# Inverse transform: token blocks joined in pairs, the residual accumulated in PSUM by ScalarE, weight splits spread over more units

## Chip, cores and metric

One core of a Trainium2 chip runs the whole program. The metric is device time in microseconds (us) of one execution. A profiled execution gives, in addition, a trace of each engine: TensorE (PE, with its weight loads shown apart as PEld), VectorE (DVE), ScalarE (ACT), GpSimd (POOL) and SyncE (SP, which here only issues DMAs). Each engine works through its own queue strictly in the order in which the program was built; engines wait for each other through semaphores.

## Reference

A layer norm of x feeds two branches, and both are added to x:

```
x: [2048 tokens, 448]            xn = layernorm(x)
A = irfft2(rfft2(xn) * (w_r + 1j*w_i))          # 2-D Fourier filter over tokens and features
B = (relu(xn @ W_gate) * (xn @ W_up)) @ W_down  # 448 -> 1792 -> 448
out = x + A + B                                  # all float32
```

## The kernel before

**Precision and TensorE work.** All matmuls run in float16 with every float32 operand split into a high and a low part (three products for one). Splitting a tile takes one ScalarE instruction (high) and one VectorE instruction (low).

**Branch B** is the foreground. F = 1792 is cut into 14 slabs f of 128, in three groups of 5, 5 and 4; the tokens are cut into four chunks q of 512. A *gu unit* (f, q) multiplies chunk q with the gate and up slab f into a pair of PSUM banks (`gu`, two pairs): `gu_full` L797 on 128 rows, `gu_half` L804 for a leftover of 64 rows, of which two units (a unit and its mate) are done side by side at the end of the earlier one, into both units' banks. Then come ReLU (`gu_relu`, ScalarE L832), gate times up (`gu_times`, VectorE L836, which is what frees the PSUM pair) and the split of the product (L840, L844). After all slabs of a group have passed for a chunk, four *dn units* multiply the products with W_down (L868), each on one of two banks `dn`; ScalarE seeds the bank with x (`dn_seed`, L861) and takes the sum out again into x (`dn_post`, L872). The last four dn units are written out by hand in `dn_end` (L900, L879). Slabs of weights are loaded into staging buffers `wst` (8 of 128x512), squared and summed for a scale, and split by `w_hi` (ScalarE L746) and `w_lo` (VectorE L750) some units before their first use.

**Branch A** is the background. Tokens are 16 blocks n2 of 128 (token 16p + n2 sits in partition p). The forward half makes, per pair of blocks n2 and n2 + 8, a transform along the features and one along the tokens of a block (matmuls `f_dft` L414 and `f_sdft` L447), and combines the 16 blocks by four stages of butterflies on VectorE in 128x464 float32 tiles `y`. After the product with w, three stages of butterflies go back. Then, for p = 0..7, the **inverse runs** that the change rewrites:

- `bring(p)`: `stage4` (`bfly`, L453 to L478) joins two tiles into blocks p and p + 8, in two tiles `y`; `i_swap` (L648) has SP copy one row `row` into the tile and exchange its partition halves into a buffer `sw` by two DMAs (L586, L587; four buffers).
- `i_pair` (L592, L593) adds the exchanged side, once for each block.
- `i_mix` (L655) is an 8-point step along the features, `eight_a` and `eight_b` (L365 to L388): 16 VectorE instructions for each block. The forward half calls the same two functions on tiles that hold two blocks (128x928, called `eo` and `bw`).
- `i_hi` (ScalarE L667) and `i_lo` (VectorE L672) split the result into `vt`; `i_sdft` (L682) transforms along the tokens into a PSUM bank `fx` (there are two), `i_pqhi` and `i_pqlo` (L688, L691) split that.
- `i_ddft` (L705) transforms p and p + 8 along the features into both `fx` banks; a one-column ScalarE copy (`two_banks`, L398) goes first. `i_acc` (VectorE L719, two instructions of 128x224 for each block) scales the sums and adds them to x in `xy`, which frees the banks. `store` sends a block to HBM once both branches are in it. Blocks whose dn bank is seeded at that moment wait for `dn_post` (the set `seeded`).

One row of frequencies takes a path of its own: `row_dft` (PE L632), `row_hi2`/`row_lo2` (L623, L627), `row_ev` (VectorE L645), whose result the swaps need.

**What sets the order.** The opening is written out as a list. After it a loop over the units issues the foreground, and `run_bg` adds background steps from the list `bg`, each with a VectorE cost in us; a load factor is solved so that the background is used up by the unit that stands LASTGU before the last gu unit. `sched` and `gslot` place weight loads and splits a number of gu units ahead. The tile framework then orders each engine's queue by its own timing model and priorities.

Of the kernel before, what the change touches and what calls it, by code (L numbers as in the profile page):

```python
# [43 lines left out]
NSW = 4  # L44
LASTGU = 5
# [39 lines left out]
def _constants():  # L85
# [46 lines left out]
    for s in range(8):  # L132
        th = 2 * np.pi * (np.outer(kp, m + s) % D) / D
        o = slice(56 * (s // 2), 56 * (s // 2) + 56)
        c_id[64 * (s % 2):64 * (s % 2) + GW, :, o] = np.stack(
            _split(np.concatenate([g * np.cos(th), -g * np.sin(th)], axis=0)), axis=1)
# [7 lines left out]
def tile_gfnet_reglu(ctx: ExitStack, tc: tile.TileContext, x, xr, wgu, wd, wf, ident, c_fd, c_fm, c_im, c_row, c_id,  # L144
# [21 lines left out]
    xy = mt([128, 16, D], F32, "xy")  # L166
# [48 lines left out]
    def load_x(n2):  # L215
        nc.sync.dma_start(xy[:, n2, :], xv[:, n2, :])
# [9 lines left out]
    def load_w(f, g, eng=nc.sync):  # L226
        wst[f, g] = mt([128, 4, 128], F32, "wst", 8)
        eng.dma_start(wst[f, g], wgu[f, :, g])
# [219 lines left out]

    def bfly(a, b, p, sgn):
# [16 lines left out]
        th = 2 * np.pi * p / 16  # L466
        c, s = float(np.cos(th)), float(np.sin(th)) * sgn
        if abs(c) >= abs(s) - 1e-9:
            k, f = s / c, c
            V.scalar_tensor_tensor(t[:, :, 0], b[:, :, 1], k, b[:, :, 0], op0=OP.mult, op1=OP.add)  # L470
            V.scalar_tensor_tensor(t[:, :, 1], b[:, :, 0], -k, b[:, :, 1], op0=OP.mult, op1=OP.add)
        else:
            k, f = c / s, s
            V.scalar_tensor_tensor(t[:, :, 0], b[:, :, 0], k, b[:, :, 1], op0=OP.mult, op1=OP.add)
            V.scalar_tensor_tensor(t[:, :, 1], b[:, :, 1], k, b[:, :, 0], op0=OP.mult, op1=OP.subtract)
# [41 lines left out]
    def wsq_scale():  # L517
# [4 lines left out]
        V.tensor_scalar(fsc[:, 1:2], n, 2.0 ** -3 * 4.0 / (S * D), None, op0=OP.mult)  # L522
        V.reciprocal(fsc[:, 0:1], small[:, 19:20])

    inv = {}

    def open_inv():
        fwd.__exit__(None, None, None)
        state["ip"] = ip = ctx.enter_context(tc.tile_pool(name="inv", bufs=1))
        state["vt"] = [ip.tile([128, 2, NG, 64], F16, name=f"vt{i}") for i in range(2)]  # L530
        for v in state["vt"]:
            G.memset(v[:, :, :, GW:], 0.0)
        state["sw"] = [ip.tile([128, NG, 2, KC], F32, name=f"sw{i}") for i in range(NSW)]
# [49 lines left out]
    def swap(key):  # L583
        t = sw[key] = state["sw"][state.setdefault("swn", 0) % NSW]
        state["swn"] += 1
        nc.sync.dma_start(t[1:64], cur[key][65:128])  # L586
        nc.sync.dma_start(t[65:128], cur[key][1:64])  # L587

    def pair(key, sgn):
        u, t = cur[key], sw.pop(key)  # L590
# [61 lines left out]
    def i_pair(n2):  # L652
        pair(("U", n2), -1)

    def i_mix(n2):  # L655

        u = cur.pop(("U", n2))
        t, s = free.pop(0), free.pop(0)
        eight_a(u, s, u[:, 1:4])
        eight_b(t, s, u[:, 1:4], -1)  # L660
        free.extend((u, s))
        cur["Q", n2] = t

    def i_hi(n2):
        v = vt[n2] = state["vt"][state.setdefault("vn", 0) % 2]
        state["vn"] += 1
        A.activation(v[:, 0, :, 0:GW], cur["Q", n2].rearrange("p g c k -> p g (c k)"), AF.Copy, scale=fsc[:, 0:1])  # L667

    def i_lo(n2):
        ut = cur.pop(("Q", n2))  # L670
        v = vt[n2]
        V.scalar_tensor_tensor(v[:, 1, :, 0:GW], ut.rearrange("p g c k -> p g (c k)"), fsc[:, 0:1], v[:, 0, :, 0:GW],  # L672
                               op0=OP.mult, op1=OP.subtract)
        free.append(ut)

    def i_sdft(n2):
        ps = fx()
        v, m = vt[n2].rearrange("p a g k -> p a (g k)"), im_t[n2]
# [351 lines left out]
    for p in range(-1, 8):  # L1030
        if p >= 0:
            both(0.6, i_pqlo, p)
        if -1 < p < 6:
            bring(p + 2)
# [282 lines left out]
```

## Time and profile before

| | |
|---|---|
| Median of 3 runs | 447.38 us (447.23 to 448.21) |
| The profiled execution | 446.98 us |
| Its span, first to last instruction | 445.2 us |
| ScalarE busy | 239.5 us, 54%, 502 instructions |
| GpSimd busy | 35.7 us, 8% |
| Idle of VectorE before L836, in all | 7.6 us, waiting for ScalarE's ReLU |
| Idle of VectorE before L592, in all | 6.4 us, waiting for the DMAs of `row` and `sw` |
| SP issues of a swap (L586, L587) | 64, 0.73 and 0.71 us each in the middle |

The span is what the engines need, and the execution has 1.8 us around it. Where rows of the profile are shown, *busy* is the time an engine has at least one instruction in flight; an instruction's own duration is longer than the distance to the next one, since they overlap. A value in square brackets behind a row is the idle time in front of it, with what ended it.

### The profile page before, as it was taken

To read this page: it belongs to the slowest core of one execution; us is meant where nothing else is said; L and a number is where in the kernel's file an instruction comes from. 1 tells how busy PE (TensorE), PEld (TensorE's weight loads), DVE (VectorE), ACT (ScalarE), POOL (GpSimd) and SP (SyncE) were. 2 spreads that over 40 slices of the span, in tenths; PEclk is the share of its full clock that TensorE was granted. 3 is DMA by queue.
4 is the path that set the end of the run, shared out by engine and by line. 5 is a ranking of instruction groups with operands and counts; after the bars stand their busy time and mean duration, and the time that the engine had idled before them with its cause. 6 is when DMAs were issued, how large, how long until landed. Compare 5 with 4: busy or idle time off the path is not lost.

```text
span 445.2 us, 8321 instructions
## 1 busy us (share of the span) xinstructions
PE 433.0 (97%) x3009; PEld 209.7 (47%) x3009; DVE 391.0 (88%) x1077; ACT 239.5 (54%) x502; POOL 35.7 (8%) x89
## 2 busy tenths in 40 slices
PE   7999999999999999999999999989999989999996
PEld 2544444444454444444444444434555544554554
DVE  5988798997998899999999999699999979997343
ACT  5888484577468837616333573573552623625440
POOL 2320040040200040000000012010000000000000
PEclk9999999999999999999999999999999999999999
DMA  7839995050002362432202100200120111120112
GB/s 258 299 83 253 383 275 103 2 101 8 2 0 72 117 202 96 137 105 86 85 2 85 44 0 1 86 1 2 55 91 8 33 64 56 45 95 12 69 63 82
DMA packets 39512, 39.66 MB, mean 89 GB/s; under 512 B 18736, under 2 KB 35376, under 8 KB 39472
## 3 DMA queue, kind: packets, MB, share of 16 engines
q1 hardware_dynamic: 39472, 39.14, 28.8%
q8 instruction: 23, 0.38, 0.4%
q14 instruction: 17, 0.14, 0.1%
HBM read 24.25 MB, written 3.67 MB: 63 GB/s over the span
## 4 chain that ended last, share of the span: by engine, by line
DVE 51%; PE 34%; DMA 5%; issue 4%; ACT 3%; SPq 1%; POOL 1%; DVEq 0%; ACTq 0%
PE gu L797 18%; PE dn L868 9%; DVE g L836 5%; DVE h L844 4%; DVE wt L750 3%; DVE y L454 2%; DVE y L478 2%; DVE y L453 2%; DMA sw<-y 2%; DVE y L593 2%; DVE y L559 2%; DVE y L556 2%; DVE y L477 2%; DVE y L592 2%; PE fx L447 1%
## 5 line engine op out<-in xcount | busy, mean ns | idle before, releaser
L797 PE MATMUL gu<-T,wt 128*128 128x512 f16 (+1 forms) x1140 | 254.1, 375 | 0.4 <-DVE wt L750 0.4
L797 PEld LDWEIGHTS <-wt 128*128 128x128 f16 x1140 | 109.1, 98 | 132.2 <-issue 9.7
L868 PE MATMUL dn<-wdt,h 128*128 128x448 f16 x624 | 127.3, 353 | 0.0
L868 PEld LDWEIGHTS <-h 128*128 128x128 f16 x624 | 59.9, 98 | 57.2 <-issue 1.3
L840 ACT ACTIVATE h<-g 128x512 f16<-128x512 f32 x56 | 35.0, 627 | 91.8 <-DVE g L836 91.7
L836 DVE SCALAR_TENSOR_TENSOR g<-gu,g 128x512 f32<-128x512 f32 x56 | 38.2, 682 | 7.6 <-ACT g L832 7.6
L832 ACT ACTIVATE g<-gu 128x512 f32<-128x512 f32 x56 | 32.8, 585 | 19.3 <-PE gu L797 11.7
L844 DVE TENSOR_TENSOR h<-g,h 128x512 f16<-128x512 f32 x56 | 38.1, 682 | 5.6 <-ACT h L840 5.5
L872 ACT ACTIVATE xy<-dn,dsc 128x448 f32<-128x448 f32 x44 | 27.4, 625 | 23.4 <-PE dn L868 23.4
L861 ACT ACTIVATE dn<-xy,dinv 128x448 f32<-128x448 f32 x44 | 27.6, 632 | 11.5 <-DVE xy L719 10.9
L191 POOL PARTITION_ALL_REDUCE wm<-wm x15 | 10.2, 679 | 162.6 <-ACT junk L188 162.6
L746 ACT ACTIVATE wt<-wst,wsc 128x512 f16<-128x512 f32 x28 | 19.3, 713 | 3.5 <-DVE wsc L198 3.5
L750 DVE SCALAR_TENSOR_TENSOR wt<-wst,wsc,wt 128x512 f16<-128x512 f32 x28 | 20.5, 746 | 0.5 <-ACT wt L746 0.4
L804 PE MATMUL gu<-T,wt 64*128 64x512 f16 x112 | 16.9, 380 | 1.6 <-DVE g L836 1.5
L592 DVE TENSOR_TENSOR y<-y,sw 128x232 f32<-128x232 f32 x32 | 12.6, 393 | 6.4 <-DMA y<-row 3.2
L188 ACT ACTIVATE junk<-wst 128x512 bf16<-128x512 f32 x28 | 17.3, 619 | 0.4 <-DMA wst<-in_wgu 0.3
L719 DVE SCALAR_TENSOR_TENSOR xy<-fx,fsc,xy 128x224 f32<-128x224 f32 x32 | 12.2, 443 | 5.1 <-PE fx L705 5.0
L252 DVE BATCH_NORM_STATS2 bst<-y 128x6 f32<-128x448 f32 x16 | 9.5, 611 | 5.7 <-DMA y<-in_xr 5.7
L667 ACT ACTIVATE vt<-y,fsc 128x464 f16<-128x464 f32 x16 | 10.8, 676 | 6.6 <-DVE y L388 5.7
L453 DVE TENSOR_TENSOR y<-y,y 128x464 f32<-128x464 f32 x22 | 14.0, 637 | 0.3
L454 DVE TENSOR_TENSOR y<-y,y 128x464 f32<-128x464 f32 x22 | 13.9, 632 | 0.0
L682 PE MATMUL fx<-im,vt 128*128 128x128 f16 x192 | 12.0, 219 | 1.4 <-DVE xy L719 1.4
(147 smaller groups left out, 515.2 us busy)
## 6 DMA issues: line engine op xcount, KB each, us to landing
sw<-y SPq DMA_DIRECT2D x64, 114.2 KB
wst<-in_wgu SPq DMA_DIRECT2D x28, 256.0 KB
wf<-in_wf SPq DMA_DIRECT2D x16, 232.0 KB
y<-in_xr SPq DMA_DIRECT2D x16, 224.0 KB
xy<-in_x SPq DMA_DIRECT2D x16, 224.0 KB
out<-xy SPq DMA_DIRECT2D x15, 224.0 KB
wdst<-in_wd SPq DMA_DIRECT2D x14, 224.0 KB
fm<-in_c_fm SPq DMA_DIRECT2D x4, 256.0 KB
```

Source lines behind the costliest of these rows:

```text
L453: V.tensor_tensor(t, a, b, op=OP.add)
L454: V.tensor_tensor(d, a, b, op=OP.subtract)
L592: V.tensor_tensor(u[:, :, 0], u[:, :, 0], t[:, :, 1], op=o1)
L750: V.scalar_tensor_tensor(w[:, 4:8, :], st, sc, w[:, 0:4, :], op0=OP.mult, op1=OP.subtract)
L797: last["P"] = P.matmul(hps[f, q][:, g, cs], wt[f, g][:, a, :], Tq[q][:, b, cs], start=(start and i == 0), stop=(stop and i == len(seq) - 1 ...
L832: last["A"] = A.activation(g1s[f, q], hps[f, q][:, 0, :], AF.Relu, scale=2.0 ** -22).ins
L836: last["V"] = V.scalar_tensor_tensor(g1, hps[f, q][:, 1, :], 2.0 ** -22, g1, op0=OP.mult, op1=OP.mult).ins
L840: A.activation(ht[f, q][:, 0, :], g1s[f, q], AF.Copy)
L844: V.tensor_tensor(h[:, 1, :], g1s.pop((f, q)), h[:, 0, :], op=OP.subtract)
L861: A.activation(dps[n2][:, 0:D], xy[:, n2, :], AF.Copy, scale=dinv[:, g:g + 1])
L868: last["P"] = P.matmul(dps[n2][:, 0:D], ht[f, q][:, a, js], wdt[f][:, b, :], start=False, stop=(f == fs[-1] and a == 1), skip_group_check= ...
L872: last["A"] = A.activation(xy[:, n2, :], dps[n2][:, 0:D], AF.Copy, scale=dsc[:, g:g + 1]).ins
```

## The change

1. **Two blocks share a tile.** `i_join` writes both results of the last butterfly into one tile of 128x928 (blocks p and p + 8 side by side), which it takes from the ring of `wst` (now 4 buffers of 128x1024 for pairs of slabs, in place of 8 single ones). `i_swap`, `i_pair`, `i_mix`, `i_hi` then work on the pair; `i_lo` has still one instruction for each block. There are two swap buffers of double size.
2. **The residual goes through PSUM.** `i_ddft` has ScalarE put x, scaled by 1/`fsc[1]`, into the two `fx` banks; the matmuls add to it, and ScalarE takes the scaled sum out into `xy`. Each of the four instructions covers both blocks (128x448), for which `xy` is laid out so that p and p + 8 are neighbours. A pair with a block in `seeded` goes the old way (`fresh`).
3. `c_id` has its sine part 32 rows below the cosine part (padding in `vt`, one tile), and its scale takes a factor 8/7.
4. **Splits spread.** `w_hi`, `w_lo` and the next load are scheduled for half g at slot + g; LASTGU goes from 5 to 9. The list `bg` is written for pairs, with costs for them.

```diff
-LASTGU = 5
+LASTGU = 9
...
+    xy2 = mt([128, 8, 2, D], F32, "xy")
+    xy = [xy2[:, n2 % 8, n2 // 8] for n2 in range(16)]
...
+        if g == 0:
+            t = mt([128, 2, 4, 128], F32, "wst", 4)
+            wst[f, 0], wst[f, 1] = t[:, 0], t[:, 1]
         eng.dma_start(wst[f, g], wgu[f, :, g])
...
-    def i_swap(n2):
-        nc.sync.dma_start(cur["U", n2][64:65], row[n2:n2 + 1])
-        swap(("U", n2))
...
+    def i_join(p):
+
+        u = U[p] = mt([128, 2, 4, 128], F32, "wst", 4).rearrange(...)
+        a, b = cur.pop(("i3", 0, p)), cur.pop(("i3", 1, p))
+        o, d = (u[:, :, :, KC * i:KC * (i + 1)] for i in range(2))
...
+            t = free.pop(0)
+            f = rotate(t, b, p, -1)
+            V.scalar_tensor_tensor(o, t, f, a, op0=OP.mult, op1=OP.add)
+            V.scalar_tensor_tensor(d, t, -f, a, op0=OP.mult, op1=OP.add)
...
+    def i_swap(p):
+        u = U[p]
+        for i in range(2):
+            nc.sync.dma_start(u[64:65, :, :, KC * i:KC * (i + 1)], row[p + 8 * i:p + 8 * i + 1])
+        t = sw[p] = state["sw"][p % 2]
+        nc.sync.dma_start(t[1:64], u[65:128])
+        nc.sync.dma_start(t[65:128], u[1:64])
...
+    def i_lo(p):
+        u, hi, lo = i_sides(p)
+        for b in range(2):
+            V.scalar_tensor_tensor(lo[:, b], u[:, b], fsc[:, 0:1], hi[:, b], op0=OP.mult, op1=OP.subtract)
...
     def i_ddft(a, b, m=None):
-        banks = two_banks()
+        fresh = a in seeded or b in seeded
+        banks = two_banks() if fresh else (fx(), fx())
+        sides = [banks[e][:, 0:D].rearrange("p (b d) -> p b d", b=2) for e in range(2)]
+        for e in range(0 if fresh else 2):
+            with tc.high_priority(offset=400):
+                A.activation(sides[e], xy2[:, a, :, 224 * e:224 * (e + 1)], AF.Copy, scale=fsc[:, 2:3])
...
+        if not fresh:
+            for e in range(2):
+                with tc.high_priority(offset=400):
+                    A.activation(xy2[:, a, :, 224 * e:224 * (e + 1)], sides[e], AF.Copy, scale=fsc[:, 1:2])
+            store(a)
+            store(b)
+            return
...
-            sched(gslot(s, 4), w_hi, f, g)
-            sched(gslot(s, 4), w_lo, f, g)
-            sched(gslot(s, 4), load_wn)
+            sched(gslot(s, 4) + g, w_hi, f, g)
+            sched(gslot(s, 4) + g, w_lo, f, g)
+            sched(gslot(s, 4) + 1, load_wn)
```

### The order at three places

Line numbers shift: `row_ev` L645 becomes L657, `gu_times` L836 becomes L891, `w_lo` L750 becomes L805, `i_pair` L592 becomes L604, the join of the last butterfly is L669 to L679. Numbers behind a name tell buffers apart.

**First place: VectorE at the last change of slab group**, from the end of one `gu_times` region to the next. Before, between `row_ev` and the `gu_times` of `gu_3510` stand both swap additions, the start of a mix and six low splits (the last part of it):

```order
L750 SCALAR_TENSOR_TENSOR wt_3556<-wst_2218,wsc_3521,wt_3556 128x512
L369 TENSOR_TENSOR y8_74<-y7_73 128x174
L198 TENSOR_SCALAR wsc_3631<-eg_89 128x2
L750 SCALAR_TENSOR_TENSOR wt_3559<-wst_2223,wsc_3521,wt_3559 128x512
L750 SCALAR_TENSOR_TENSOR wt_3625<-wst_2261,wsc_3562,wt_3625 128x512
L370 TENSOR_TENSOR y7_73<-y7_73 128x174
L384 TENSOR_TENSOR y13_79<-y8_74 128x58
L385 TENSOR_TENSOR y13_79<-y8_74 128x58
L750 SCALAR_TENSOR_TENSOR wt_3628<-wst_2266,wsc_3562,wt_3628 128x512
L377 TENSOR_TENSOR y7_73<-y7_73 128x2x29
L836 SCALAR_TENSOR_TENSOR g1_3593<-gu_3510,g1_3593 128x512
```

In the changed kernel the same unit is `gu_3466`, and this is what stands in front of its `gu_times`:

```order
L805 SCALAR_TENSOR_TENSOR wt_3519<-wst_2194,wsc_3316,wt_3519 128x512
L805 SCALAR_TENSOR_TENSOR wt_3522<-wst_2236,wsc_3474,wt_3522 128x512
L669 TENSOR_TENSOR wst_3490<-y7_73,y2_68 128x16x29
L670 TENSOR_TENSOR wst_3490<-y7_73,y2_68 128x16x29
L805 SCALAR_TENSOR_TENSOR wt_3566<-wst_2236,wsc_3474,wt_3566 128x512
L805 SCALAR_TENSOR_TENSOR wt_3569<-wst_2296,wsc_3525,wt_3569 128x512
L657 TENSOR_SCALAR row_86<-fx_3485,small_87 16x8x29 x2
L891 SCALAR_TENSOR_TENSOR g1_3534<-gu_3466,g1_3534 128x512
```

`row_ev` moved from far ahead of this `gu_times` to directly in front of it; the swap additions and the mix moved behind it, as did three of the eight low splits.

**Second place: ScalarE around `i_ddft` of the third pair of blocks** (p = 2). Before, with the split of the token transform (L688), one dn unit's exit and entry, and the one-column copy:

```order
L667 ACTIVATE vt0_2287<-y4_70,fsc_88 128x8x58
L688 ACTIVATE wf_4242<-fx_4216 128x512
L840 ACTIVATE h_4305<-g1_4302 128x512
L667 ACTIVATE vt1_2288<-y10_76,fsc_88 128x8x58
L688 ACTIVATE wf_4244<-fx_4229 128x512
L872 ACTIVATE xy_61<-dn_4308,dsc_91 128x448
L861 ACTIVATE dn_4394<-xy_61,dinv_92 128x448
L398 ACTIVATE fx_4324<-eps_93 128x1
L872 ACTIVATE xy_61<-dn_4310,dsc_91 128x448
```

Now (L729 is the split, L927 and L916 exit and entry of a dn unit, L743 the entry and L759 the exit of `i_ddft`, L710 `i_hi` of the next pair):

```order
L729 ACTIVATE wf_4165<-fx_4139 128x512
L729 ACTIVATE wf_4167<-fx_4152 128x512
L927 ACTIVATE xy_61<-dn_4285,dsc_91 128x448
L916 ACTIVATE dn_4307<-xy_61,dinv_92 128x448
L743 ACTIVATE fx_4206<-xy_61,fsc_88 128x448
L927 ACTIVATE xy_61<-dn_4287,dsc_91 128x448
L743 ACTIVATE fx_4207<-xy_61,fsc_88 128x448
L710 ACTIVATE vt_2359<-wst_3959,fsc_88 128x32x29
L916 ACTIVATE dn_4364<-xy_61,dinv_92 128x448
L759 ACTIVATE xy_61<-fx_4207,fsc_88 128x2x224
L759 ACTIVATE xy_61<-fx_4206,fsc_88 128x2x224
```

Four instructions of 448 columns took the place of the copy of one column; the dn exits and entries stand between them.

**Third place: VectorE at the end of that pair.** Before, the exit of the `i_ddft` banks (L719) stands behind a swap addition of a later pair and the tail of two mixes:

```order
L592 TENSOR_TENSOR y2_68<-y2_68,sw3_2294 128x8x29
L593 TENSOR_TENSOR y2_68<-y2_68,sw3_2294 128x8x29
L387 SCALAR_TENSOR_TENSOR y13_79<-y11_77 128x2x58
L388 SCALAR_TENSOR_TENSOR y13_79<-y11_77 128x2x58
L387 SCALAR_TENSOR_TENSOR y5_71<-y15_81 128x2x58
L388 SCALAR_TENSOR_TENSOR y5_71<-y15_81 128x2x58
L719 SCALAR_TENSOR_TENSOR xy_61<-fx_4325,fsc_88,xy_61 128x224
L719 SCALAR_TENSOR_TENSOR xy_61<-fx_4324,fsc_88,xy_61 128x224 x2
L836 SCALAR_TENSOR_TENSOR g1_4598<-gu_4507,g1_4598 128x512
```

Now the stretch in front of the `gu_times` of the same unit (`gu_4469`) has no exit of a bank in it; further ahead in this stretch the swap addition (L604) follows its join at these rows:

```order
L678 SCALAR_TENSOR_TENSOR wst_4352<-y2_68,y0_66 128x16x29
L899 TENSOR_TENSOR h_4282<-g1_4279,h_4282 128x512
L679 SCALAR_TENSOR_TENSOR wst_4352<-y2_68,y0_66 128x16x29
L390 SCALAR_TENSOR_TENSOR wst_3959<-wst_4264 128x2x116
L732 SCALAR_TENSOR_TENSOR wf_4165<-fx_4139,wf_4165 128x512
L732 SCALAR_TENSOR_TENSOR wf_4167<-fx_4152,wf_4167 128x512
L391 SCALAR_TENSOR_TENSOR wst_3959<-wst_4264 128x2x116
L368 TENSOR_TENSOR wst_4436<-wst_4169 128x2x232
L370 TENSOR_TENSOR wst_4436<-wst_4169 128x2x2x116
L372 TENSOR_TENSOR wst_4169<-wst_4436 128x348
L604 TENSOR_TENSOR wst_4352<-wst_4352,sw1_2362 128x8x58
```

L719 moved from VectorE to ScalarE (L759 above). Only four L719-like instructions remain on VectorE (one pair, p = 6, goes the old way).

More of the change, by code (lines that the diff above doesn't have):

```diff
@@ L215, in load_x @@
     def load_x(n2):
[L216 removed]
+        nc.sync.dma_start(xy[n2], xv[:, n2, :])
     def load_xr(n2):
@@ L1023, in bring @@
     def bring(p):
-        add(bf[p], stage4, p, -1, "i3", "U")
-        both(0.0, i_swap, p)
+        add(bf[p], i_join, p)
+        add(0.0, i_swap, p)
     bring(0)
-    both(0.62, i_pair, 0)
+    add(1.1, i_pair, 0)
     bring(1)
@@ L1032, in tile_gfnet_reglu @@
             both(0.6, i_pqlo, p)
-        if -1 < p < 6:
-            bring(p + 2)
+        if p >= 0:
+            add(0.0, i_ddft, p, p + 8)
         if p < 6:
@@ L1037, in tile_gfnet_reglu @@
         if p < 7:
-            add(2.47, i_mix, p + 1)
-        if p >= 0:
-            add(0.0, i_ddft, p, p + 8)
-        if p < 7:
-            add(2.47, i_mix, p + 9)
-            both(0.0, i_hi, p + 1)
-        if p >= 0:
-            both(0.6, i_acc, p)
-        if p < 6:
-            both(0.62, i_pair, p + 2)
-        if p < 7:
-            both(0.6, i_lo, p + 1)
+            add(1.97, i_mix, p + 1, 0)
+            add(2.1, i_mix, p + 1, 1)
+            add(0.0, i_hi, p + 1)
+        if p < 6:
+            add(1.1, i_pair, p + 2)
+        if p < 7:
+            add(1.1, i_lo, p + 1)
             both(0.0, i_sdft, p + 1)
             both(0.0, i_pqhi, p + 1)
+        if p < 5:
+            bring(p + 3)
     pos = [0]
```

122 lines of the change are left out of this document (69 added, 53 removed).

## The prediction

> **What bounds the kernel now.** I read the page first: who is busy, and what the chain that ended last is made of.
>
> ```profile
> span 445.2 us, 8321 instructions
> PE 433.0 (97%) x3009; PEld 209.7 (47%) x3009; DVE 391.0 (88%) x1077; ACT 239.5 (54%) x502; POOL 35.7 (8%) x89
> DVE 51%; PE 34%; DMA 5%; issue 4%; ACT 3%; SPq 1%; POOL 1%; DVEq 0%; ACTq 0%
> ```
>
> TensorE is busy for 433.0 of 445.2 us. The chain gives VectorE half of the span, but where two engines are both nearly full a chain may run along either. So the next view is busy time by stretches of the program; the columns are length, PE, PEld, DVE, ACT, POOL, each with its count, then granted clock, DMA share and GB/s.
>
> ```profile
> 0.00:22.26 22.26, 18.03 (x115) 9.76 (x116) 16.91 (x57) 15.85 (x36) 6.49 (x26) 1.00 0.82 278
> 22.26:278.25 255.99, 255.56 (x1608) 118.09 (x1606) 238.97 (x592) 150.23 (x328) 27.05 (x61) 1.00 0.34 98
> 278.25:300.51 22.26, 20.36 (x103) 9.54 (x102) 17.93 (x50) 14.38 (x31) 2.15 (x3) 1.00 0.14 43
> 300.51:356.16 55.65, 55.65 (x416) 28.21 (x414) 55.07 (x187) 26.74 (x49) 0.00 (x0) 1.00 0.12 38
> 356.16:378.42 22.26, 20.53 (x206) 10.17 (x205) 19.12 (x75) 6.99 (x14) 0.00 (x0) 1.00 0.19 60
> 378.42:441.30 62.88, 62.82 (x571) 33.95 (x568) 42.15 (x120) 25.31 (x47) 0.00 (x0) 1.00 0.15 51
> 441.30:445.20 3.90, 0.00 (x0) 0.00 (x0) 0.86 (x3) 0.00 (x0) 0.00 (x0) 1.00 0.61 219
> ```
>
> The clock is 1.00 throughout. TensorE idles 4.2 us in the opening and 3.9 us after its last matmul. Between these it idles only in two stretches of 22 us: 1.90 us in one, 1.73 in the other, and 0.49 in the rest. VectorE is full where the inverse runs begin (55.07 of 55.65 us) and has 20.7 us to spare in the last 63. I then looked, in TensorE's timeline, for where it waited in the two stretches; start, busy time, instruction, and in brackets the idle time in front.
>
> ```profile
> 282.13 0.36 PE L632 MATMUL fx<-rowh,row_t 128*128 128x232 f16 x2 [0.38 <-DVE rowh L627]
> 297.13 0.61 PE L804 MATMUL gu<-T,wt 64*128 64x512 f16 x4 [1.52 <-DVE g L836]
> 363.93 1.51 PE L682 MATMUL fx<-im,vt 128*128 128x128 f16 x24 [1.44 <-DVE xy L719]
> 372.97 0.80 PE L705 MATMUL fx<-idc_t,wf 64*128 64x56 f16 x48 [0.19 <-DVE wf L691]
> ```
>
> These four waits are all that VectorE costs TensorE after the opening, 3.53 us together. TensorE's records overlap, though:
>
> ```profile
> L797 PE MATMUL gu<-T,wt 128*128 128x512 f16 (+1 forms) x1140 | 254.1, 375 | 0.4 <-DVE wt L750 0.4
> 63.17 4.32 PE gu L797 x20
> ```
>
> In the chain 20 such matmuls take 4.32 us, 0.216 each, while one record lasts 0.375. A wait breaks an overlap of 0.16 us, so four waits cost 3.53 + 4 x 0.16 = **4.2 us**. That is the most that the change can bring: the matmuls after it are the same in number and shape, and opening and tail are built as before.
>
> **The change, part by part.** *VectorE's relief.*
>
> ```profile
> L719 DVE SCALAR_TENSOR_TENSOR xy<-fx,fsc,xy 128x224 f32<-128x224 f32 x32 | 12.2, 443 | 5.1 <-PE fx L705 5.0
> L365 DVE TENSOR_TENSOR y<-y 128x232 f32<-128x232 f32 x16 | 6.2, 390 | 0.0
> L365 DVE TENSOR_TENSOR bw<-eo 128x464 f32<-128x464 f32 x8 | 5.1, 636 | 5.6 <-ACT eo L419 5.6
> L377 DVE TENSOR_TENSOR y<-y 128x58 f32<-128x58 f32 x32 | 6.7, 210 | 0.0
> L377 DVE TENSOR_TENSOR eo<-bw 128x116 f32<-128x116 f32 x8 | 2.2, 270 | 0.0
> ```
>
> The accumulation goes down from 32 instructions to 4: 28 x 0.443 = 12.4 us. For the mix, two instructions become one of double size, and the forward half already has that size: 2 x 0.390 becomes 0.636, 2 x 0.210 becomes 0.270. That saves 0.14 to 0.15 us each time; a block has 16, so 8 pairs save about 128 x 0.145 = 18.6 us of durations. Like TensorE's, these overlap. By busy time over count (6.2/16, 6.7/32, 5.1/8) hardly, but within a run of instructions starts lie some 0.08 us closer than ends, and 155 instructions fewer also take 155 such overlaps away. So of 12.4 + 18.6 + some 2.4 for the swap additions I count 33 - 155 x 0.08, about 20 us, an estimate; some three quarters of it falls behind the last change of slab group at 278 us.
>
> *The wait at 297 us.* What stood in front of it on VectorE:
>
> ```profile
> 290.07 0.40 DVE L592 TENSOR_TENSOR y<-y,sw 128x232 f32<-128x232 f32 x1 [3.16 <-DMA y<-row]
> 292.67 0.74 DVE L750 SCALAR_TENSOR_TENSOR wt<-wst,wsc,wt 128x512 f16<-128x512 f32 x1
> 293.65 1.40 DVE L750 SCALAR_TENSOR_TENSOR wt<-wst,wsc,wt 128x512 f16<-128x512 f32 x2
> 295.49 0.74 DVE L750 SCALAR_TENSOR_TENSOR wt<-wst,wsc,wt 128x512 f16<-128x512 f32 x1
> 296.39 0.69 DVE L836 SCALAR_TENSOR_TENSOR g<-gu,g 128x512 f32<-128x512 f32 x1
> 291.52 0.58 ACT L832 ACTIVATE g<-gu 128x512 f32<-128x512 f32 x1
> ```
>
> ReLU had ended at 292.1; the product began at 296.4, behind four low splits and pieces of a mix, after VectorE had lost 3.16 us on a swap. In the new order two low splits and half a join stand there, and the addition comes behind the product. TensorE waited 1.52; some 4 us of work leave its way, so it goes: 1.68. What is late next there is `row_ev`, now directly ahead of this product (first rival).
>
> *The wait at 364 us* is for a bank that two accumulations had to empty, and these stood behind a swap addition that waited:
>
> ```profile
> 361.32 0.40 DVE L592 TENSOR_TENSOR y<-y,sw 128x232 f32<-128x232 f32 x1 [0.81 <-DMA sw<-y]
> 362.71 1.52 DVE L719 SCALAR_TENSOR_TENSOR xy<-fx,fsc,xy 128x224 f32<-128x224 f32 x4
> ```
>
> ScalarE, which now empties the banks, waits for no swap: 1.60 goes. The waits at 282 and 373 us (0.54 and 0.35) are for splits that come late on a full VectorE; the row transform now stands behind more foreground matmuls, and VectorE has less to do. I take them as gone as well.
>
> *What ScalarE gets.*
>
> ```profile
> L861 ACT ACTIVATE dn<-xy,dinv 128x448 f32<-128x448 f32 x44 | 27.6, 632 | 11.5 <-DVE xy L719 10.9
> L872 ACT ACTIVATE xy<-dn,dsc 128x448 f32<-128x448 f32 x44 | 27.4, 625 | 23.4 <-PE dn L868 23.4
> ```
>
> Seven pairs bring two seeds and two exits each: 28 x 0.63 = 17.6 us, of the same form and size as these rows, on an engine with 54% of its time used and 25.31 of 62.88 in the last stretch. Beside other work that costs nothing. On the path it may stand once per pair: the seeds, if they come later than the last product that TensorE has queued; the exits, if the next transform wants the bank. Ends: nothing, or 7 x 4 x 0.63 = 17.6 us. In the order, foreground matmuls lie between; by their count at 0.216 us I get 4 us and more between a `i_ddft` and the next `i_sdft`, where two exits need 1.3. I take 0.
>
> *Splits spread and LASTGU:* the same instructions elsewhere. In the middle TensorE idles 0.43 us of 255.99, so nothing is to be won there; moved splits may cost it: I put 0 to 1 us, and take 0.3, about one of the waits seen. *Double tiles* alter where VectorE waits for a transfer:
>
> ```profile
> sw<-y SPq DMA_DIRECT2D x64, 114.2 KB
> wf<-in_wf SPq DMA_DIRECT2D x16, 232.0 KB
> 323.48 2.86 DMA sw<-y
> 238.14 2.60 DMA wf<-in_wf
> ```
>
> No row has a swap of 228 KB. Its landing lies between a gain of 0.3 us (a load of 232 KB took 2.60 where a swap of 114 KB took 2.86) and a loss of 2.86 (twice the time). The rows are nearest to no change, as 114 and 232 KB differ so little, and issues halve, so I take 0. The tightest pair has some 3.3 us of VectorE work between join and addition, against about 5 for row copy, issue and landing: VectorE idles some 1.7 us for it, which its spare 20 us cover.
>
> **Sum:** -1.68 - 1.60 - 0.54 - 0.35 = -4.2, and +0.5 for splits moved and a small new wait: -3.7. From the profiled 446.98 that makes 443.3. This execution lies 0.4 below the median of the runs shown, 447.38, so against the median I say **443.6 us**.
>
> **The rivals.** *First: the inverse runs start late (445.4).* TensorE's first inverse matmul stood at 312.7:
>
> ```profile
> L682 PE MATMUL fx<-im,vt x192: 219/219/230, 312.7 to 428.1; 128*128 128x128 f16 x192
> 307.31 0.69 DVE L672 SCALAR_TENSOR_TENSOR vt<-y,fsc,vt 128x464 f16<-128x464 f32 x1
> 285.21 0.91 DVE L645 TENSOR_SCALAR row<-fx,small 16x232 f32<-16x232 f32 x2
> ```
>
> Its input was ready at 308.0, 4.7 us ahead. With the row transform placed later, `row_ev` waits (by the matmuls in front) until about 289 instead of 285, and everything in front of the first `i_sdft` shifts: I get a slack of about 1.2 us. If a swap takes 1 to 3 us longer, TensorE waits about 1.8 there: 443.6 + 1.8 = 445.4. For: the thinnest hand-over of the new order. Against: slack is still above zero by every row.
>
> *Second: ScalarE takes VectorE's place (446.9).* If in front of each of seven pairs one instruction (0.63 less a little) is on TensorE's way, 7 x 0.47 = 3.3 us come back: 443.6 + 3.3 = 446.9. For: `dn_seed`, `dn_post`, `i_hi`, `i_pqhi` and ReLU share that queue. Against: 40% busy in the last stretch. The Trainium skill speaks for this rival (ScalarE: Activation LUTs, "Rules for kernel authors"): plain adding and multiplying belongs on VectorE. Here that would give back the 12.4 us on VectorE; the rows show 0.443 twice per block there against 0.63 twice here, a loss only where ScalarE is on the path.
>
> *Third, slower (448.7): the double swap lands late.* One swap now covers a pair, with nothing of the other block to do meanwhile.
>
> ```profile
> L592 DVE TENSOR_TENSOR y<-y,sw 128x232 f32<-128x232 f32 x32 | 12.6, 393 | 6.4 <-DMA y<-row 3.2 <-DMA sw<-y 3.1
> ```
>
> VectorE now idles 6.4 us for swaps and 5.1 for sums, and gains some 15 us of work behind 278 us: 26.5 us in all. Over the six pairs after the first two it is worse off than before from 26.5 / 6 = 4.4 us of idling per pair. At twice the 2.86 us of landing, and half an us more for issues of double size, it idles 1.7 + 2.86 + 0.5 = 5.0 per pair, 30.4 us, and ends 3.9 us later than now. Only the two waits ahead of the pairs are then saved, and TensorE waits for the rest: 447.4 - 1.68 - 0.54 + 3.9 = 449.1, less what slack takes up, some 0.4: 448.7. For: VectorE is saturated from 300 to 356. Against: 232 KB in 2.60. The Trainium skill states a rule that would favour it (DMA: Bandwidth & Descriptors, "Why a DMA increments its semaphore by 16 and not by 1"): a transfer is cut over the largest number up to 16 that divides its slowest dimension, for the 63 partitions here 9. An estimate by its 27 GiB/s per engine adds some 0.45 us to a swap of double size, which is short of what decides; no row here shows how many engines a swap used.
>
> *Fourth: no effect (447.2).* The waits were only where VectorE's lateness came out, and it comes out elsewhere. Against: 20 us of spare time at the end, and ScalarE takes over the bank.
>
> **How the numbers follow.** Forecast 0.50; first rival 0.17; second 0.15; slower 0.13; no effect 0.05. A measurement of this kernel tells about 0.2%, 0.9 us, from no change. The forecast and the first rival are faster (0.67, with a rest of 0.01 from the fourth), the second and fourth within 0.2% (0.18 together, after that rest and a part of the second that lies below), the third slower, with a rest of the others: 0.14. The range: below, all 4.2 us and another 1 us of spread between executions (447.23 to 448.21 before), 447.4 - 5.2 = 442.2; above, the second rival and half an us, 447.6.
>
> **What would show it.** Right: TensorE gapless from 22 us on; no wait at the last change of group; ScalarE's exits of `fx` done before the next `i_sdft`; VectorE with some 20 us less busy time and no wait in front of `gu_times`. First rival: a wait of TensorE on the first `i_sdft` for `i_lo`. Second: waits of `i_ddft` or `i_sdft` for ScalarE. Third: idle time of VectorE in front of the swap additions of over 4 us per pair, and waits of TensorE between 300 and 380 us. The forecast is wrong if TensorE's waits after the opening add up to more than 2 us.

## The result, and the profile after

| | before | after |
|---|---|---|
| Median of 6 runs each | 447.31 us (446.83 to 448.21) | 444.00 us (443.54 to 444.21) |
| Ratio | | 0.9924, 95% interval 0.9911 to 0.9937 |
| The profiled execution | 446.98 us | 444.21 us |

The changed kernel is 0.8% faster, 3.4 us by the ratio; 443.6 was forecast. First the page of the changed kernel: span, busy time, the chain that ended last.

```profile
span 442.4 us, 8132 instructions
PE 431.8 (98%) x3009; PEld 209.9 (47%) x3009; DVE 375.7 (85%) x922; ACT 254.0 (57%) x515; POOL 39.7 (9%) x84
PE 76%; DVE 13%; DMA 6%; issue 1%; SPq 1%; ACT 0%; POOL 0%; DVEq 0%; ACTq 0%
```

TensorE has the same 3009 matmuls. VectorE is busy for 15.3 us less, ScalarE for 14.5 us more, and the chain runs over TensorE for three quarters of the span, where it ran over VectorE for half. The same stretches as before, with the same columns:

```profile
278.25:300.51 22.26, 22.26 (x113) 10.51 (x111) 19.87 (x46) 14.90 (x32) 0.84 (x2) 1.00 0.13 43
300.51:356.16 55.65, 55.65 (x460) 28.43 (x458) 49.16 (x117) 32.23 (x54) 0.00 (x0) 1.00 0.15 46
356.16:378.42 22.26, 20.64 (x180) 10.76 (x178) 20.83 (x52) 8.91 (x16) 0.00 (x0) 1.00 0.21 63
378.42:438.70 60.28, 60.20 (x541) 32.09 (x538) 30.02 (x58) 30.72 (x52) 0.00 (x0) 1.00 0.13 45
```

The 1.90 us of TensorE's idle time at the change of group are gone. From 300 to 356 us VectorE, which had been full, has 6.5 us to spare. The stretch from 356 us still has 1.62 us of TensorE idling. TensorE's timeline says where:

```profile
364.48 4.48 PE L852 MATMUL gu<-T,wt 128*128 128x512 f16 x20 [1.19 <-DVE g L891]
369.84 0.80 PE L753 MATMUL fx<-idc_t,wf 64*128 64x56 f16 x48 [0.31 <-ACT fx L743]
```

Of four waits with 3.53 us, two with 1.50 us are left, and both are new. The longer is for gate-times-up. Its place in VectorE's timeline:

```profile
351.26 0.52 DVE L372 TENSOR_TENSOR wst<-wst 128x348 f32<-128x348 f32 x1
354.15 0.64 DVE L604 TENSOR_TENSOR wst<-wst,sw 128x464 f32<-128x464 f32 x1 [2.37 <-DMA sw<-wst]
...
363.55 0.27 DVE L388 TENSOR_TENSOR wst<-wst 128x116 f32<-128x116 f32 x1
363.74 0.68 DVE L891 SCALAR_TENSOR_TENSOR g<-gu,g 128x512 f32<-128x512 f32 x1
```

VectorE waits 2.37 us for a swap, then works without a gap through the pieces of a mix, and gate-times-up stands behind the last of them. Three of the pairs' swaps in the chain of waits (start of the second of the two issues, time from there to the landing), and the group of the swap additions of the pairs:

```profile
318.07 4.23 DMA sw<-wst
349.78 4.24 DMA sw<-wst
360.04 5.14 DMA sw<-wst
L604 DVE TENSOR_TENSOR wst<-wst,sw 128x464 f32<-128x464 f32 x8 | 5.1, 638 | 5.1 <-DMA sw<-wst 5.1
```

A single swap had landed in 2.86 us, measured the same way. The double one takes 1.4 to 2.3 us longer, and all 5.1 us of VectorE's waiting for the pairs' swaps stand at three of the eight.

### The profile page after: what moved, and what is told of

It is laid out like the page before. It is cut to its first block, busy times and chain, and to the rows that moved or that the text cites. A ratio compares the mean times of both kernels' runs of the same rounds, so it can differ in the third digit from the quotient of the medians.

```text
span 442.4 us, 8132 instructions
## 1 busy us (share of the span) xinstructions
PE 431.8 (98%) x3009; PEld 209.9 (47%) x3009; DVE 375.7 (85%) x922; ACT 254.0 (57%) x515; POOL 39.7 (9%) x84
## 4 chain that ended last, share of the span: by engine, by line
PE 76%; DVE 13%; DMA 6%; issue 1%; SPq 1%; ACT 0%; POOL 0%; DVEq 0%; ACTq 0%
PE gu L852 43%; PE dn L923 23%; DMA sw<-wst 3%; PE gu L859 3%; DMA wst<-in_wgu 2%; PE fx L450 2%; DVE vt L715 1%; PE fx L417 1%; DVE g L891 1%; PE fx L723 1%; DMA y<-in_xr 1%; DVE h L899 1%; PE dn L955 1%; DVE wst L604 1%; PE fx L753 1%
## 5 line engine op out<-in xcount | busy, mean ns | idle before, releaser
L891 DVE SCALAR_TENSOR_TENSOR g<-gu,g 128x512 f32<-128x512 f32 x56 | 38.4, 685 | 18.6 <-ACT g L887 18.4
L927 ACT ACTIVATE xy<-dn,dsc 128x448 f32<-128x448 f32 x44 | 27.6, 629 | 25.0 <-PE dn L923 24.9
L192 POOL PARTITION_ALL_REDUCE wm<-wm x15 | 16.0, 1072 | 155.8 <-ACT junk L189 155.8
L916 ACT ACTIVATE dn<-xy,dinv 128x448 f32<-128x448 f32 x44 | 27.6, 632 | 0.5
L805 DVE SCALAR_TENSOR_TENSOR wt<-wst,wsc,wt 128x512 f16<-128x512 f32 x28 | 20.6, 748 | 1.0 <-ACT wt L801 1.0
L732 DVE SCALAR_TENSOR_TENSOR wf<-fx,wf 128x512 f16<-128x512 f32 x16 | 10.9, 688 | 4.9 <-ACT wf L729 4.9
L440 ACT ACTIVATE Xh<-eo 128x464 f16<-128x464 f32 x16 | 8.9, 596 | 8.7 <-DVE eo L391 8.7
L710 ACT ACTIVATE vt<-wst,fsc 128x928 f16<-128x928 f32 x8 | 8.8, 1097 | 8.6 <-DVE wst L391 6.1
L470 DVE TENSOR_TENSOR y<-y,y 128x464 f32<-128x464 f32 x21 | 13.4, 637 | 0.2
L471 DVE TENSOR_TENSOR y<-y,y 128x464 f32<-128x464 f32 x21 | 13.3, 636 | 0.0
L723 PEld LDWEIGHTS <-vt 128*128 128x128 f16 x192 | 11.4, 98 | 2.0 <-issue 0.4
```

The source lines that it names most:

```text
L805: V.scalar_tensor_tensor(w[:, 4:8, :], st, sc, w[:, 0:4, :], op0=OP.mult, op1=OP.subtract)
L891: last["V"] = V.scalar_tensor_tensor(g1, hps[f, q][:, 1, :], 2.0 ** -22, g1, op0=OP.mult, op1=OP.mult).ins
L916: A.activation(dps[n2][:, 0:D], xy[n2], AF.Copy, scale=dinv[:, g:g + 1])
L927: last["A"] = A.activation(xy[n2], dps[n2][:, 0:D], AF.Copy, scale=dsc[:, g:g + 1]).ins
```

## The experiments

Each was timed in five rounds beside the kernel before, whose median in these groups was 446.2 to 446.6 us; so ratios are compared (the changed kernel's row is the result above). *Idle* sums TensorE's waits behind the opening in the timeline and the waits view (without 0.4 us at 35 us, which every version has). *First* is the start of the first `i_sdft`.

| Kernel | us | ratio (95%) | idle, us | first, us |
|---|---|---|---|---|
| before | | 1 | 3.53 | 312.7 |
| changed kernel | 444.00 | 0.9924 (0.9911 to 0.9937) | 1.50 | 311.5 |
| ScalarE's sum alone | 441.82 | 0.9894 (0.9873 to 0.9916) | 0 | 320.2 |
| joined tiles alone | 455.44 | 1.0215 (1.0182 to 1.0247) | 9.9 | 327.7 |
| spread and LASTGU 9 alone | 451.80 | 1.0112 (1.0091 to 1.0134) | 5.3 | 295.0 |
| spread alone | 445.22 | 0.9965 (0.9948 to 0.9983) | 2.1 | 310.9 |
| changed, without ScalarE's sum | 450.11 | 1.0080 (1.0058 to 1.0101) | 4.8 | 312.2 |
| changed, without joined tiles | 448.27 | 1.0042 (1.0024 to 1.0059) | 4.1 | 306.5 |
| changed, without spread and LASTGU 9 | 449.39 | 1.0060 (1.0039 to 1.0081) | 5.7 | 327.7 |
| changed, LASTGU 5 | 448.11 | 1.0038 (1.0022 to 1.0054) | 5.6 | 328.0 |
| changed, rows behind swaps | 444.27 | 0.9951 (0.9933 to 0.9969) | 1.45 | 311.7 |
| changed, 48 of 63 rows exchanged | 442.14 | 0.9901 (0.9882 to 0.9921) | 0 | 311.5 |
| changed, swaps twice | 454.53 | 1.0178 (1.0154 to 1.0202) | 9.2 | 311.5 |
| changed, swaps cut in 48 and 15 | 442.23 | 0.9907 (0.9889 to 0.9925) | 0 | 311.7 |

### One part alone, one part out

The theory was that each part takes away one wait. The rival was that any relief of VectorE does.

**ScalarE's sum alone**: the kernel before with point 2 of the change (`xy` with neighbours, seeds and exits in `i_ddft`, `i_acc` only for pairs with a seeded block).

```diff
-        banks = two_banks()
+        fresh = a in seeded or b in seeded
+        banks = two_banks() if fresh else (fx(), fx())
...
-            both(0.6, i_acc, p)
+            both(0.0, i_acc, p)
```

> The kernel before with the accumulation by ScalarE alone: single tiles and swaps, splits and LASTGU as before. Theory (each part takes away one wait): the bank wait of 1.44 us at 364 goes, the wait at the change of group stays: 445.2 to 446.2 against 447.3. Rival (the joined tiles bring the gain): 446.9 to 447.5; second rival of the prediction (ScalarE on TensorE's path): 447 or more, with waits of i_ddft for the seeds.

It is the fastest kernel of the study. Its timeline has no wait of TensorE behind the opening; two stretches of its windows:

```profile
280.00:300.00 20.00, 20.00 (x101) 9.32 (x99) 17.55 (x40) 14.66 (x31) 1.08 (x2) 1.00 0.08 25
360.00:380.00 20.00, 20.00 (x194) 10.79 (x187) 18.97 (x60) 13.27 (x23) 0.00 (x0) 1.00 0.13 43
```

So all of the waits go, the one at the change of group too, where the theory let it stand. The order moved with the edit: the sums are off the planner's list of VectorE work, and the inverse runs start at 320.2 in place of 312.7. Which of the two took the waits away, the engine of the sums or the later start, isn't shown: no run starts the kernel before that late with its sums on VectorE. ScalarE never stands in TensorE's way here. The Trainium skill has a rule against this part (ScalarE: Activation LUTs, "Rules for kernel authors": adding and multiplying on VectorE). On this kernel the measurement decides for ScalarE, by 1.1%: VectorE is the engine with too little room, and the sum costs ScalarE 32 instructions of 0.63 us here (28 in the changed kernel), for which TensorE doesn't wait.

**Joined tiles alone**: the changed kernel with the next two diffs undone together.

> The kernel before with joined tiles and double swaps alone (the changed kernel without the accumulation by ScalarE and without spread splits). Theory (each part takes away one wait): both waits of about 1.5 us stay, and double swaps come later, 446.5 to 448.5 against 447.3 of before. Rival (the joined tiles bring the gain): 444 to 445.

**Without ScalarE's sum**:

```diff
-        fresh = a in seeded or b in seeded
+        fresh = True
```

> The changed kernel with the residual added by VectorE for every pair, as for the pairs with a seeded block: 28 instructions of 0.44 us back on VectorE, 28 of 0.63 off ScalarE. Theory (each part takes away one wait; a bank that ScalarE empties does not wait behind a swap): TensorE waits for a bank behind VectorE's sums again, 1.5 us or more, some of it at several pairs: 445.5 to 447. Rival (VectorE has time enough, the joined tiles do it): 443.7 to 444.5.

**Without the fourth part**:

```diff
-LASTGU = 9
+LASTGU = 5
-            sched(gslot(s, 4) + g, w_hi, f, g)
+            sched(gslot(s, 4), w_hi, f, g)
```

(`w_lo` and `load_wn` likewise.)

> The changed kernel with its fourth part undone: low and high splits of both halves of a slab in the same unit again, LASTGU 5. Theory (each part takes away one wait; splits in front of gate-times-up at the change of group made the wait of 1.5 us at 297): that wait comes back wholly or in part, 444.9 to 445.7 against 444.0. Rival (any relief of VectorE does it, the parts are interchangeable): no wait at the change of group, 443.7 to 444.3.

All three are slower than the kernel before, by 0.6 to 2.2%, all beyond what either theory gave. The joined tiles, which save VectorE most, are by themselves a loss. Its size needs care: the background list of the changed kernel has no entry for the sums, which the kernel before plans at 0.6 us of VectorE for each block. With joined tiles alone and without ScalarE's sum, VectorE therefore does 32 sums (12.2 us) that the planner doesn't count. Joined tiles without this difference are seen between ScalarE's sum alone (0.9894) and the changed kernel without the fourth part (1.0060): there they cost 1.7%.

TensorE's timeline with joined tiles alone, and two stretches of its windows (the granted clock is the third number from the end):

```profile
376.33 0.80 PE L753 MATMUL fx<-idc_t,wf 64*128 64x56 f16 x48 [3.85 <-DVE wf L732]
377.64 6.07 PE L852 MATMUL gu<-T,wt 128*128 128x512 f16 x20 [0.52 <-DVE g L891]
404.75 2.73 PE L723 MATMUL fx<-im,vt 128*128 128x128 f16 x24 [2.23 <-DVE xy L774]
```

```profile
376.40:379.00 2.60, 2.08 (x52) 1.23 (x52) 2.60 (x9) 1.11 (x2) 0.00 (x0) 0.71 0.00 0
379.00:382.00 3.00, 3.00 (x11) 1.10 (x10) 2.97 (x9) 0.63 (x1) 0.00 (x0) 0.68 0.01 1
```

Two things stand here. The waits are now 2 to 4 us, for splits and sums of a pair, at the end of a pair's long chain (join, swap, addition, mix, split). VectorE waits 12.5 us for the pairs' swaps, at five places, and the chain in front of the wait of 3.85 us begins with a swap that took 5.44 us to land. That two separate blocks would have filled these gaps for each other is argued, not measured. And after a long wait the clock falls: 20 matmuls take 6.07 us where they took 4.48 after the wait of 1.19 us in the changed kernel. The same without ScalarE's sum:

```profile
373.84 1.03 PE L859 MATMUL gu<-T,wt 64*128 64x512 f16 x4 [2.13 <-DVE g L891]
374.81 6.43 PE L852 MATMUL gu<-T,wt 128*128 128x512 f16 x20
```

**Spread and LASTGU 9 alone** (the fourth part on the kernel before), and **spread alone** (with LASTGU left at 5):

> The kernel before with the spread splits and LASTGU 9 alone. Theory (each part takes away one wait): the wait of 1.52 us at the change of group goes, the others stay: 445.5 to 446.2 against 447.3. Rival (VectorE is full without the other parts, so lateness comes out elsewhere): 446.9 to 448.5.

> The kernel before with spread splits alone, LASTGU 5. Theory (of the fourth part alone, 451.8, the earlier deadline made the loss, since it starts the inverse runs at 295 in place of 313 with VectorE full; spreading itself does little): 444.5 to 446.6 beside a before of 446.2, the wait of 1.5 us at the change of group gone. Rival (the moved splits make the loss): 448 to 452.

The fourth part alone lies beyond both of its expectations; spread alone lies where its theory had it. Spreading takes the wait at the change of group from 1.52 to 0.40 us and is worth 0.35%. The earlier deadline is what turns that into a loss of 1.1%. Its rows of the first and last `i_sdft`, and the worst of its waits:

```profile
L682 PE MATMUL fx<-im,vt x192: 216/219/311, 295.0 to 423.2; 128*128 128x128 f16 x192
344.28 1.04 PE L682 MATMUL fx<-im,vt 128*128 128x128 f16 x10 [2.00 <-DVE vt L672]
```

The inverse runs start 18 us sooner, on a VectorE that is full, and TensorE waits in nine places, mostly for splits.

**The changed kernel with LASTGU 5**, and **without joined tiles** (ScalarE's sum, spread splits and LASTGU 9 on single tiles):

```diff
-LASTGU = 9
+LASTGU = 5
```

> The changed kernel with LASTGU 5 in place of 9, splits spread. Theory (the earlier deadline is what the joined tiles need: the inverse runs start 16 us sooner with it, and a pair is a longer chain than two blocks were): the first i_sdft stands near 328, TensorE waits in the last runs as without the whole fourth part, 448 to 450.5 beside a before of 446.2. Rival (it is the spreading of splits): 443.5 to 445.

> The kernel before with the accumulation by ScalarE, spread splits and LASTGU 9; single tiles and swaps: the changed kernel without joined tiles. Theory (joined tiles and their double swaps cost the changed kernel the waits that it still has): no wait of TensorE after the opening, 441.3 to 442.3 beside a before of 446.2. Rival (with single tiles the earlier deadline fills VectorE too soon, as where the fourth part stood alone, 451.8): 443.5 to 447, with waits of i_sdft for i_lo between 290 and 350.

With joined tiles the same deadline acts the other way. At LASTGU 5 the runs start at 328:

```profile
L723 PE MATMUL fx<-im,vt x192: 216/219/229, 328.0 to 435.5; 128*128 128x128 f16 x192
399.22 0.80 PE L753 MATMUL fx<-idc_t,wf 64*128 64x56 f16 x48 [2.06 <-ACT fx L743]
```

The runs take as long as with LASTGU 9 (107 us from the first `i_sdft` to the last) but end 17 us later, and the span is 4.1 us longer (446.5 for 442.4). The seed at 399 us is only the last link of its wait. ScalarE had idled in front of it:

```profile
398.53 0.64 ACT L743 ACTIVATE fx<-xy,fsc 128x448 f32<-128x448 f32 x1 [1.67 <-DVE wf L732]
```

The bank was free only after VectorE's split L732, and the chain in front of this split begins with a swap that took 5.42 us to land. Why the later runs meet more of such waits isn't shown. Without joined tiles LASTGU 9 costs as it did alone: the expectation of 441.3 to 442.3 for that kernel was wrong, its rival right, though with another wait (2.78 us, at 319.6, for a seed of a dn bank on ScalarE, which stood behind a split that had waited for VectorE).

### What is left in the changed kernel

**Rows behind swaps**: the two row copies of a pair are issued after its swaps.

```diff
-        for i in range(2):
-            nc.sync.dma_start(u[64:65, ...], row[p + 8 * i:p + 8 * i + 1])
         t = sw[p] = state["sw"][p % 2]
         nc.sync.dma_start(t[1:64], u[65:128])
         nc.sync.dma_start(t[65:128], u[1:64])
+        for i in range(2):
+            nc.sync.dma_start(u[64:65, ...], row[p + 8 * i:p + 8 * i + 1])
```

> The changed kernel with the two row copies issued behind the two swaps of a pair, not ahead of them. Theory (what is left of waiting, 1.19 + 0.31 us at 364 to 370, comes from swaps that land late and put VectorE behind): swaps leave SP 1.2 us earlier, VectorE idles about 1.2 us less at each of the pairs where it waits, TensorE's rest of waiting halves or goes: 442.8 to 443.5. Rival (gate-times-up stands behind 17 pieces of a mix by the order alone): 443.7 to 444.3.

A miss: the wait of 1.19 us stayed. VectorE's timeline tells why:

```profile
353.78 0.64 DVE L604 TENSOR_TENSOR wst<-wst,sw 128x464 f32<-128x464 f32 x1 [2.52 <-DMA wst<-row]
```

The addition needs swap and row; with the order turned it waits as long for the row, which now queues behind the swaps. The run doesn't tell lateness from order.

**48 of 63 rows exchanged** (15 rows of each side are left out, so this kernel serves for the measurement alone):

```diff
-        nc.sync.dma_start(t[1:64], u[65:128])
-        nc.sync.dma_start(t[65:128], u[1:64])
+        nc.sync.dma_start(t[1:49], u[65:113])
+        nc.sync.dma_start(t[65:113], u[1:49])
```

> The changed kernel with 48 of 63 partitions exchanged in each swap; 15 rows of each side are left out. The place of gate-times-up among the pieces of the mix stays as it is. Theory on the landing (a swap over 63 partitions runs on 9 engines, 7 rows of 0.145 us each; over 48 on 16, 3 rows each): the landing of two swaps falls from 4.24 by about 1.2 us to some 3.1. Rival (the bytes decide): it falls by 24% of what the bytes take, 0.3 to 0.5 us, to 3.8. Theory on the time (late swaps put VectorE behind): TensorE's wait of 1.19 us at 364 goes or halves, 442.6 to 443.4; rival (the order alone): 443.7 to 444.3.

This does. VectorE's order around gate-times-up is as in the changed kernel, the addition comes 2.7 us sooner (351.43 for 354.15), and TensorE's wait is gone:

```profile
347.40 0.58 SPq L688 DMA_DIRECT2D sw<-wst  x1
351.43 0.64 DVE L604 TENSOR_TENSOR wst<-wst,sw 128x464 f32<-128x464 f32 x1 [1.14 <-DMA sw<-wst]
361.03 0.68 DVE L891 SCALAR_TENSOR_TENSOR g<-gu,g 128x512 f32<-128x512 f32 x1
```

From the start of the first issue to the addition it is 4.03 us, in the changed kernel 5.20 (348.95 to 354.15); 0.4 of the 1.17 us are shorter issues. From the start of the second issue to the addition it is 3.40 us for 4.37, so the landing took about 3.3 us, between the theory's 3.1 and the rival's 3.8. The rows of both swaps, by the DMA records of the traces, took 1.94 us (348.65 to 350.59) in place of 3.32 (350.37 to 353.70); 24% fewer bytes at the old rate would have made 2.5.

How many engines carried the data is seen in the DMA view of the two swaps, the mean busy share of 16 engines in tenths, first the changed kernel (349.7 to 354), then this one (347.9 to 351):

```profile
DMA  0000009366626584514455267545120001800000
```

```profile
DMA  0110000007964999798639939735732010000000
```

Over 63 partitions mostly 4 to 6 tenths are busy, and 9 of 16 would be 5.6; over 48 it is mostly 7 to 9, though single slices lie outside in both. The packets are clearer. In the same view (for 48 partitions from 348.5 to 352 us) stand, beside the 126 and 96 rows, 18 and 32 packets under 512 B: 9 and 16 for each swap.

```profile
DMA packets 145, 0.48 MB, mean 113 GB/s; under 512 B 18, under 2 KB 18, under 8 KB 144
DMA packets 128, 0.36 MB, mean 102 GB/s; under 512 B 32, under 2 KB 32, under 8 KB 128
```

That agrees with the rule of the Trainium skill cited in the prediction (the largest divisor up to 16). The estimate from that page, 0.45 us more per swap (0.9 for the two of a pair, if they share these engines), was too small: the landing took 1.4 us more and over.

**Swaps twice** (both swaps of a pair issued again into the same buffer):

> The changed kernel with each pair's two swaps issued twice into the same buffer, so that a pair's exchange ends some 4 to 6 us later. It prices the third rival of the prediction: at over 4.4 us of VectorE's idling per pair the change should lose what it gained. By that sum VectorE idles 5 to 7 us at six pairs, 30 to 42 us, and the time is 448 to 456. Rival (VectorE has slack enough in the last 60 us, only the pairs up to 380 us count): 444.5 to 447.

VectorE waits 13.9 us for the pairs' swaps in place of 5.1, at four places, and the span grows by 10.6 us (453.0 for 442.4); two more gaps in front of such additions, 1.44 and 0.48 us, have no cause in the view. The time lies in the theory's range, the idling far below its 30 to 42 us. The chain of waits shows the second pair of transfers behind the first:

```profile
322.00 4.25 DMA sw<-wst
326.26 4.04 DMA sw<-wst
```

**Swaps cut in 48 and 15**, all rows exchanged:

```diff
-        nc.sync.dma_start(t[1:64], u[65:128])
-        nc.sync.dma_start(t[65:128], u[1:64])
+        for i, n in ((1, 48), (49, 15)):
+            nc.sync.dma_start(t[i:i + n], u[i + 64:i + 64 + n])
+            nc.sync.dma_start(t[i + 64:i + 64 + n], u[i:i + n])
```

> The changed kernel with each of a pair's two exchanges cut into 48 and 15 partitions (four transfers for two), all rows exchanged. Theory (a transfer over 63 partitions uses 9 engines, over 48 uses 16, and late swaps are what is left): data lands sooner by about 1.4 us, two more issues cost 1.2 of it; from the first issue to the addition 5.2 falls to 4.3 to 5.0, TensorE's 1.19 us falls by some 0.3 to 0.8: 442.6 to 443.4 beside a before of 446.2. Rival (issues eat it): 443.5 or more.

TensorE's waits are gone, and it is better than expected, but not only by the landing. Where it still waits, VectorE waits 1.73 us, hardly less than the 1.81 at that pair in the changed kernel; from the first issue to the addition it is 4.78 us there (318.44 to 323.22) for 5.25 (317.24 to 322.49). At 352 us, the place of the 2.37 us, it is the order that changed:

```profile
350.96 1.31 DVE L716 SCALAR_TENSOR_TENSOR vt<-wst,fsc,vt 128x464 f16<-128x464 f32 x2
352.19 0.51 DVE L372 TENSOR_TENSOR wst<-wst 128x348 f32<-128x348 f32 x1
352.62 0.63 DVE L678 SCALAR_TENSOR_TENSOR wst<-y,y 128x464 f32<-128x464 f32 x1
353.17 0.63 DVE L679 SCALAR_TENSOR_TENSOR wst<-y,y 128x464 f32<-128x464 f32 x1
```

The framework, which now counts four transfers, put low splits and the next join ahead of the addition, where the changed kernel has nothing left to do. How much of the time the sooner landing brought by itself wasn't separated.

## Why the prediction was right, and where not

**The bound.** The change could bring TensorE's four waits, 4.2 us, and no more. The kernels without waits lie at 0.989 to 0.991, 4.2 to 4.7 us below before, at the bound within their intervals. The measured 444.0 us beside the forecast 443.6 is this bound less what is left of waits.

Some of that closeness is luck. The sum gave -3.7 us from one profiled execution to the next, and the two profiles differ by 2.8. The kernel before had a median of 447.31 us in the rounds of the result and of 446.2 to 446.6 in those of the experiments; against these the changed kernel's 444.00 would be a gain of 0.5 to 0.6%.

**The four waits that were to go.** The wait at the change of group is gone, and so is the one for the row transform. The bank is no longer waited for at 364 us. The fourth, 0.19 us in front of an `i_ddft` at 373 us, has a successor: at 370 us TensorE waits 0.31 us for a seed of ScalarE. That is all that came of the second rival (446.9), and ScalarE wasn't busy even then; it waited itself for VectorE to split what stood in the bank:

```profile
369.15 0.64 ACT L743 ACTIVATE fx<-xy,fsc 128x448 f32<-128x448 f32 x1 [0.67 <-DVE wf L732]
```

**The term that was mis-sized** is the landing of the double swap. Its bounds were -0.3 and +2.86 us, and I took 0, by the load of 232 KB from HBM that took 2.60. Measured: +1.4 to +2.3. The near row was of another kind: a load from HBM, not an exchange between partitions. VectorE waits 2.37 us for it where 1.7 was said to be the worst, and this reaches TensorE. So the +0.5 us for new waits is 1.50 us of idle time, and with two broken overlaps of 0.16 some 1.8. That makes -2.4 by the prediction's own sum; the span fell by 2.8 (445.2 to 442.4). The rest of 0.4 lies in small gaps that I can't place.

**VectorE's relief** was forecast at 20 us of busy time and is 15.3; ScalarE's load at 17.6 and is 14.5. What is left of TensorE's waiting stands at two places and doesn't follow from either size. One sign of being right failed: VectorE was to have no wait in front of `gu_times`. It had 7.6 us there and has 18.4 now:

```profile
DVE g L891 <- ACT g L887: 18.4, 8, 4.9
```

VectorE is ready before ReLU more often than it was. This idling costs nothing in itself, as TensorE waits for gate-times-up only once.

**The first rival** (445.4) stayed away: the first `i_sdft` started at 311.5, and its low split ended at 310.3, the slack of 1.2 us that was worked out.

**What the prediction had wrong without harm to its number** is how the parts stand to each other. Spread splits and LASTGU were entered at 0.3 us, as the same instructions elsewhere. Without LASTGU 9 the changed kernel is 0.4% slower than before, while on single tiles the same deadline costs 1.5% (the fourth part alone, 1.0112, against spread alone, 0.9965; with ScalarE's sum, where spreading came along, 1.0042 against 0.9894). Joined tiles were entered as the larger part of 20 us of relief; alone they lose 2.2% (1.7% where ScalarE's sum is in both kernels). I added up busy time where the hand-overs between engines decide. That these two parts balance each other in the changed kernel wasn't foreseen; that the number held in spite of it is luck.

**The third rival** (448.7) had a sound mechanism and a wrong price. It pooled VectorE's idling over all pairs against all that was saved, and set the point at 4.4 us at each of six pairs, 26.5 us. With swaps twice 13.9 us in all cost 10.6 us of span, part of it by a lower clock after two waits of TensorE of over 4 us (20 matmuls took 6.16 us behind one of them). Lateness at one pair isn't paid from room at the end, since TensorE needs the pair when its matmuls come.

## What to carry to other kernels

Time the parts of a change one by one: here one of three held all of the gain (0.989 alone, 0.992 with the others), and the two others only mended each other. Joining tiles saves instructions, but may take away the second piece of work that covered a transfer (VectorE idled 14.3 us for all swaps with joined tiles alone, 6.4 before); look at what the engine does between the issue and the use before counting what it saves. Where a planner spreads background work, its deadline is part of every change to that work: 295 us was too early for single tiles and 328 too late for joined ones.

## What the runs showed of the hardware

**A wait can cost more than itself.** After eight of the ten waits of 2.0 us and more TensorE's granted clock fell to 0.50 to 0.55 in windows of 1 to 2 us; 20 matmuls took 6.1 to 6.4 us for 4.5. So against the span of 440.0 us with ScalarE's sum alone, which has no such waits, 4.8 us of idling make 8.6 (changed, without ScalarE's sum: 448.6) and 9.9 make 14.1 (joined tiles alone: 454.1). Broken overlaps of 0.16 us are in these figures, an estimated 0.5 and 1.0 us, and some tenths from the opening; the rest is mostly the clock. Without ScalarE's sum:

```profile
374.00:376.00 2.00, 2.00 (x7) 0.44 (x4) 2.00 (x7) 1.05 (x2) 0.00 (x0) 0.50 0.00 0
376.00:378.00 2.00, 2.00 (x6) 0.76 (x5) 2.00 (x7) 0.00 (x0) 0.00 (x0) 0.50 0.00 0
```

After waits of 1.2 to 1.7 us it stayed at 1.00. It did so too after the first of two waits without ScalarE's sum (2.04 us, at 371 us) and after the wait of 2.06 us with LASTGU 5:

```profile
399.20:402.00 2.80, 2.78 (x58) 1.67 (x58) 2.80 (x8) 1.12 (x2) 0.00 (x0) 1.00 0.00 0
```

The Trainium skill (TensorE: Matmul & The Clock Gate, "What's actually happening") has the clock go to half after an idle window of about 3.4 us that runs freely. The halved clock agrees, and so does the fact that waits of nearly one length differ; but here waits of 2.0 to 2.2 us were already enough at times.

**More engines, slower packets.** The swaps' rows of 3712 bytes took 0.145 us each (medians, by the traces' DMA records) over 63 partitions, where at most 12 were in flight at a time, and 0.17 to 0.20 us over 48, with up to 18 in flight. So for the two swaps of a pair the rate rose from 141 GB/s (126 rows in 3.32 us) to 184 (96 in 1.94), by 1.3 where the engines rose by 16 to 9.
